# Starting TensorE's attention loop at step 0, on zeroed buffers, in a decode kernel that streams 186 MB

## The chip, the cores and the metric

The kernel runs on one core of a Trainium2 chip. The metric is the device time of one execution in microseconds (us), as the median of several. The profile is one further execution. Its span leaves out some 1.8 us that the device time includes.

The engines have short names in the profile. PE is TensorE, PEld its weight loads, DVE VectorE, ACT ScalarE, POOL GpSimd and SP SyncE, which issues the loads here. A core has 16 DMA engines, which carry out the loads.

## The reference, cut to what matters

One token goes through a transformer block with adaptive layer norm. All weights and the cache are read once, in bf16.

```python
mod = (silu(c) @ w_mod).reshape(1, 6, 1, -1)            # w_mod 1024 x 6144
h = layernorm(x) * (1 + ca) + sa
q = h @ wq                                              # wq 1024 x 4096, 32 heads of 128
scores = q . k_cache * 128 ** -0.5                      # 4 kv heads, 65,536 keys of 128, 8 query heads each
o = softmax(scores) . v_cache
x = x + ga * (o @ wo)
h = layernorm(x) * (1 + cb) + sb
x = x + gb * ((gelu(h @ w_gate) * (h @ w_up)) @ w_down) # F = 3584
```

K and V are 67 MB each, and the weights 51 MB.

## The kernel before

SyncE issues every load in one fixed order into ten buffers ("slots") of 2 MB: Wmod, Wq, then 32 K chunks and 32 V chunks, then Wo, gate, up and down. K chunk i uses slot i % 4, and V chunk j slot 4 + j % 4. A load is issued once TensorE has released the slot's earlier content:

```python
def issue_ready():
    while issued[0] < len(loads):
        j = loads[issued[0]]
        if j.prev is not None:
            if j.prev.freed is None:
                return
            SP.wait(j.prev.freed)
        sp.dma_start(j.view, j.src).then_inc(j.tok[0], 16)
        issued[0] += 1
```

The attention is a pipeline over 32 chunks. In step i TensorE transposes K chunk i (`T`, four groups of 16 tiles), multiplies chunk i-1 by q (`QK`), and multiplies V chunk i-2 by the softmax weights (`PV`). Steps 0 to 3 are unrolled code, because chunks -1 and -2 don't exist. Steps 4 to 31 are a hardware loop of 7 passes with 4 steps each, on TensorE alone. The other engines' code is fully unrolled. Steps 32 and 33 are unrolled again.

```python
FIRST, LAST = SITES, NC                     # 4, 32
[...]
def QK(b):
    j = i - 1
    if not 0 <= j < NC:
        return
[...]
PE.wait(t1, v_negi, v_q)
for i in range(FIRST):
    pe_step(i)
    others_step(i)
it0, it1 = FIRST // SITES, LAST // SITES
with nc.Fori(it0, it1, engines=OrderedEngineSet([pe.engine]), head_slot={pe.engine: 0}) as it:
    [...]
    for i in range(FIRST, FIRST + SITES):
        pe_step(i)
```

The products with Wmod, Wq, Wo, gate, up and down (`matvec`) take one matmul for each 128 x 128 block of the weights. The block is the stationary operand and one activation column moves.

## Time and profile before

| | before |
|---|---|
| time, median of 3 | 443.99 us (443.78 to 444.12) |
| span of the profile | 442.7 us |
| load queue (q1), share of 16 DMA engines' span | 98.5% |
| TensorE busy | 335.0 us, 76% |
| VectorE, ScalarE, GpSimd busy | 164.8, 143.1, 3.8 us |
| instruction queue (q8) | 25 packets, 0.41 MB |

The page of the kernel before gives the DMA queues with packets, MB and share of the 16 engines' span:

```profile
q1 hardware_dynamic: 15328, 185.61, 98.5%
q8 instruction: 25, 0.41, 0.3%
HBM read 185.60 MB, written 0.00 MB: 419 GB/s over the span
```

The table of stretches gives, for each: its bounds, its length, the busy time of PE, PEld, DVE, ACT and POOL with instruction counts, then the granted clock, the DMA share and GB/s. Three stretches of the kernel before:

```profile
0.00:10.00 10.00, 2.06 (x52) 1.92 (x52) 1.40 (x11) 1.46 (x2) 3.21 (x20) 1.00 0.81 317
60.00:70.00 10.00, 9.20 (x180) 8.64 (x178) 7.31 (x7) 1.88 (x1) 0.00 (x0) 1.00 1.01 429
200.00:240.00 40.00, 37.72 (x785) 37.02 (x784) 19.31 (x30) 17.86 (x73) 0.00 (x0) 0.71 1.01 432
```

The loads run at a share of 1.0 from 10 us on, at 420 to 436 GB/s. TensorE is nearly as busy in the attention (37.7 of 40 us in the last line), so the page's 76% hides a close second bound. The loads still come first: TensorE waits 15 times for a V chunk, 20.9 us in all.

In SyncE's timeline each line is one load, with its start and the length of the issue. These are the first loads of the kernel before that had to wait for the attention (K4, V2, K5, V3):

```profile
64.39 0.33 SPq L212 DMA_DIRECT2D slot<-in_A_k_cache_dram  x1
64.76 0.43 SPq L212 DMA_DIRECT2D slot<-in_A_v_cache_dram  x1
70.41 0.33 SPq L212 DMA_DIRECT2D slot<-in_A_k_cache_dram  x1
70.78 0.43 SPq L212 DMA_DIRECT2D slot<-in_A_v_cache_dram  x1
```

The last pieces of the chain of waits before (start, length, what) show how the kernel ends. The last down-projection load lands at 439.23 us, and 3.4 us of small work follow:

```profile
414.49 24.74 DMA slot<-in_B_w_down_dram
439.23 0.05 issue
439.28 0.60 PE kt_ps L316 x16
```

### The profile page before, as it was taken

What the parts mean: (1) busy time and instruction counts of PE and PEld (TensorE: products, weight loads), DVE (VectorE), ACT (ScalarE), POOL (GpSimd) and SP (SyncE); (2) the same over time, 40 slices, a digit from 0 to 9 for tenths busy, and PEclk for the clock granted to TensorE, in tenths of its full rate; (3) what the DMA queues carried; (4) which work ended last, traced back from release to release, by engine and by line L of the source; (5) the groups of instructions that cost most, each with busy time, mean ns of one, the idle gap of its engine ahead of it and who ended that gap; (6) DMA issues with size and microseconds to landing.
All of it is one profiled execution on the core that took longest, in us unless ns stands there. A gap on an engine that the chain in (4) does not pass through costs nothing.

```text
span 442.7 us, 16779 instructions
## 1 busy us (share of the span) xinstructions
PE 335.0 (76%) x7849; PEld 325.2 (73%) x7849; DVE 164.8 (37%) x282; ACT 143.1 (32%) x548; POOL 3.8 (1%) x21
## 2 busy tenths in 40 slices
PE   1333468898979899989899988979898974654434
PEld 1333458898979899979799987969898964654434
DVE  1000046544536445544644644554544443210000
ACT  1000013444444333634533453543343562000000
POOL 2000000000000000000000000000000000000000
PEclk9999999867788956967955996895967785555555
DMA  8999999999999999999999999999999999999994
GB/s 329 429 423 426 434 431 426 429 427 421 432 429 432 426 427 437 432 429 428 434 434 430 429 429 433 431 434 429 429 434 431 432 429 428 423 424 424 427 425 177
DMA packets 15392, 186.08 MB, mean 420 GB/s; under 512 B 1536, under 2 KB 1536, under 8 KB 3840
## 3 DMA queue, kind: packets, MB, share of 16 engines
q1 hardware_dynamic: 15328, 185.61, 98.5%
q8 instruction: 25, 0.41, 0.3%
q14 instruction: 7, 0.06, 0.0%
q10 hardware_dynamic: 32, 0.00, 0.0%
HBM read 185.60 MB, written 0.00 MB: 419 GB/s over the span
## 4 chain that ended last, share of the span: by engine, by line
DMA 75%; PE 20%; issue 2%; DVE 1%; SPq 1%; ACT 1%
DMA slot<-in_A_v_cache_dram 55%; PE kt_ps L417 9%; DMA slot<-in_A_wq_dram 8%; DMA slot<-in_B_w_up_dram 6%; DMA slot<-in_B_w_down_dram 6%; PE b L481 5%; PE sc_ps L437 3%; PE kt_ps L316 1%; SPq L212 1%; PE b L461 1%; ACT p_sb L547 1%; PE b L451 1%; DVE kt_sb L612 0%; PE b L621 0%; DVE zs L597 0%
## 5 line engine op out<-in xcount | busy, mean ns | idle before, releaser
L417 PE MATMUL kt_ps<-ident,slot 128*128 128x128 bf16 x2048 | 171.9, 252 | 4.9 <-DMA slot<-in_A_k_cache_dram 3.0
L516 DVE COPY kt_sb<-kt_ps 128x2048 bf16<-128x2048 bf16 x96 | 117.5, 1225 | 100.0 <-PE kt_ps L417 99.7
L417 PEld LDWEIGHTS kt_ps<-ident,slot 128*128 128x128 bf16 x2048 | 148.6, 114 | 6.6 <-issue 4.2
L516 ACT ACTIVATE kt_sb<-kt_ps 128x2048 bf16<-128x2048 bf16 x32 | 60.1, 1878 | 217.7 <-PE kt_ps L417 217.7
L481 PE MATMUL b<-p_sb,slot 128*128 128x8 bf16 x2048 | 71.0, 167 | 29.5 <-DMA slot<-in_A_v_cache_dram 20.9
L481 PEld LDWEIGHTS b<-p_sb,slot 128*128 128x128 bf16 x2048 | 65.1, 100 | 32.2 <-DMA slot<-in_A_v_cache_dram 22.2
L547 ACT ACTIVATE p_sb<-sc_ps,mneg 128x64 bf16<-128x64 f32 x256 | 83.6, 560 | 5.7 <-DVE mneg L542 5.7
L547 ACT ACTIVATION_READ_ACCUMULATOR p_sb<-sc_ps,mneg 128x1 f32 x256 | 77.2, 364 | 0.0
L437 PE MATMUL sc_ps<-q_buf,kt_sb 128*128 128x8 bf16 x2048 | 67.4, 167 | 0.1
L437 PEld LDWEIGHTS sc_ps<-q_buf,kt_sb 128*128 128x128 bf16 x2048 | 65.1, 100 | 0.2 <-issue 0.2
L316 PE MATMUL kt_ps<-h_col,slot 128*128 128x1 bf16 x448 | 16.2, 172 | 16.9 <-DMA slot<-in_B_w_up_dram 9.1
L316 PEld LDWEIGHTS kt_ps<-h_col,slot 128*128 128x128 bf16 x448 | 15.6, 118 | 17.6 <-DMA slot<-in_B_w_up_dram 9.4
L316 PE MATMUL sc_ps<-s_col,slot 128*128 128x1 bf16 x384 | 11.5, 165 | 15.8 <-DMA slot<-in_w_mod_dram 15.8
L535 DVE TENSOR_REDUCE m_col<-sc_ps 128x8 f32<-128x512 f32 x32 | 21.8, 681 | 4.4 <-PE sc_ps L437 4.4
L316 PEld LDWEIGHTS sc_ps<-s_col,slot 128*128 128x128 bf16 x384 | 11.0, 105 | 16.4 <-DMA slot<-in_w_mod_dram 16.4
L540 DVE TENSOR_REDUCE mg<-b 8x1 f32<-8x128 f32 x32 | 8.9, 279 | 34.4 <-PE b L451 34.4
L316 PE MATMUL sc_ps<-h_col,slot 128*128 128x1 bf16 x256 | 7.4, 165 | 12.6 <-DMA slot<-in_A_wq_dram 12.6
L316 PEld LDWEIGHTS sc_ps<-h_col,slot 128*128 128x128 bf16 x256 | 7.1, 104 | 12.9 <-DMA slot<-in_A_wq_dram 9.3
L461 PE MATMUL b<-negi,mg 8*128 8x8 f32 x64 | 15.0, 304 | 0.4 <-DVE mg L540 0.4
L461 PEld LDWEIGHTS b<-negi,mg 8*128 8x128 f32 x64 | 12.0, 233 | 2.6 <-DVE mg L540 0.6
L316 PE MATMUL kt_ps<-u_col,slot 128*128 128x1 bf16 x224 | 6.6, 165 | 9.6 <-DMA slot<-in_B_w_down_dram 9.6
L316 PEld LDWEIGHTS kt_ps<-u_col,slot 128*128 128x128 bf16 x224 | 6.3, 104 | 9.9 <-DMA slot<-in_B_w_down_dram 6.8
(74 smaller groups left out, 63.2 us busy)
## 6 DMA issues: line engine op xcount, KB each, us to landing
slot<-in_A_k_cache_dram SPq DMA_DIRECT2D x32, 2048.0 KB, 29.6
slot<-in_A_v_cache_dram SPq DMA_DIRECT2D x32, 2048.0 KB, 33.2
slot<-in_w_mod_dram SPq DMA_DIRECT2D x8, 1536.0 KB, 19.0
slot<-in_A_wq_dram SPq DMA_DIRECT2D x4, 2048.0 KB, 37.0
slot<-in_A_wo_dram SPq DMA_DIRECT2D x4, 2048.0 KB, 34.7
slot<-in_B_w_gate_dram SPq DMA_DIRECT2D x4, 1792.0 KB, 39.4
slot<-in_B_w_up_dram SPq DMA_DIRECT2D x4, 1792.0 KB, 29.0
slot<-in_B_w_down_dram SPq DMA_DIRECT2D x3, 2048.0 KB, 30.4
```

Of the source, the lines that this page charges most:

```text
L212: sp.dma_start(j.view, j.src).then_inc(j.tok[0], 16)
L316: ins = pe.matmul(bank[:, j:j + 1], w, rhs[:, k0 + kk:k0 + kk + 1], start=first, stop=True, skip_group_check=True,)
L417: ins = pe.transpose(kt_ps[:, half * 2048 + t * P:half * 2048 + (t + 1) * P], j_k[i].view[:, b * TB + t, :], ident[:, :],)
L437: ins = pe.matmul(sc_ps[:, base + n * REP:base + (n + 1) * REP], kt_sb[:, j % 2, n, :], q_buf[:, j % SITES, :], start=True, stop=True,)
L451: ins = pe.transpose(b6[0:REP, 32:32 + P], m_col[:, j % 2, :], identf[:, :]) if emit else None
L461: ins = pe.matmul(b6[:, 256:256 + REP], mg8[:, j % 2:j % 2 + 1].to_broadcast([REP, P]), negi[:, :], start=True, stop=True,)
L481: ins = pe.matmul(b7[:, s * REP:(s + 1) * REP], j_v[j].view[:, n, :], p_sb[:, s, n, :], start=(n == 0), stop=(n == CH - 1),)
L516: ev[i % SITES][b].done(act.activation(dst, src, ACT.Copy) if E_ is AC else dve.tensor_copy(dst, src))
L535: m1[s].done(dve.tensor_reduce(m_col[:, j % 2, :].unsqueeze(2), scv, AX.X, ALU.max))
L540: m2[s].done(dve.tensor_reduce(mg8[:, j % 2:j % 2 + 1], b6[0:REP, 32:32 + P], AX.X, ALU.max))
L547: ins = act.activation(p_sb[:, s, :, h], scv[:, h, :], ACT.Exp, bias=mneg[:, j, h:h + 1], scale=scale, accum_out=z_all[:, j, h:h + 1],)
```

## The change

The intent is a shorter TensorE program. The loop covers steps 0 to 31 in 8 passes, and the four unrolled steps ahead of it go. In the first pass, chunks -1 and -2 are buffers of zeros: half of `kt_sb`, two of the four places of `p_sb`, and half of `m_col` and of `mg8`. V chunks -2 and -1 are whatever lies in slots 6 and 7. These hold the first two Wq loads, which therefore may not be overwritten until steps 0 and 1 have read them (times zero). Results of the first pass that no one needs are written over later. The diff, cut to its core:

```diff
--- before
+++ after
@@ loads planned
-        j_k, j_v = {}, {}
+        j_k, j_v = {}, {-2: j_q[0][0], -1: j_q[1][0]}
@@ constants on GpSimd
         v_const = GP.done(ins)
+        GP.wait(v_const)
+        pool.memset(kt_sb[:, 1, :, :], 0.0)
+        pool.memset(p_sb[:, SITES - 2:SITES, :, :], 0.0)
+        pool.memset(m_col[:, 1, :], 0.0)
+        v_zero = GP.done(pool.memset(mg8[:, 1:2], 0.0))
@@ matvec(..., held=())
-                release(jb, tok)
+                if jb not in held:
+                    release(jb, tok)
@@ the Wq product
-        v = matvec(acc_bank["q"], with_view(j_q), h_col, (v_h,), HQ)
+        v = matvec(acc_bank["q"], with_view(j_q), h_col, (v_h,), HQ, held=(j_v[-2], j_v[-1]))
@@ range of the loop
-        FIRST, LAST = SITES, NC
+        FIRST, LAST = 0, NC
@@ T, QK, MT, MB, PV: the guard (five times alike; cut)
-                if not 0 <= j < NC:
+                if j >= NC:
                     return
@@ PV
-                            b7[:, s * REP:(s + 1) * REP], j_v[j].view[:, n, :], p_sb[:, s, n, :],
+                            b7[:, s * REP:(s + 1) * REP], kv_view(slots[SITES + s])[:, n, :], p_sb[:, s, n, :],
@@ ahead of the loop
-        PE.wait(t1, v_negi, v_q)
-        for i in range(FIRST):
-            pe_step(i)
-            others_step(i)
+        PE.wait(t1, v_negi, v_q, v_zero)
[... two waits, in T and PV, lose their "i >= 1" and "j >= 1" ...]
```

TensorE's program so loses 576 matmuls and a few small ones, each with a weight load. No other engine's order changes, except for the four memsets on GpSimd.

More of the change, by code (lines that the diff above doesn't have):

```diff
@@ L304, in emit_all, with matvec @@
         v_s = DVE.done(dve.tensor_tensor(s_col[:, :], b6[:, 0:KD], sg_col[:, :], ALU.mult))
-        def matvec(bank, jobs, rhs, ready, nblk, pick=None, first=True):
+        def matvec(bank, jobs, rhs, ready, nblk, pick=None, first=True, held=()):
             PE.wait(*ready)
@@ L404, in T @@
             def T(b):
-                if not 0 <= i < NC:
+                if i >= NC:
                     return
@@ L411, in T @@
                     pwait(ev[s][b - 2], i, it)
-                elif i >= 1:
+                else:
                     pwait(ev[(i - 1) % SITES][b + 2], i - 1, it)
@@ L447, in MT @@
                 j = i - 1
-                if not 0 <= j < NC:
+                if j >= NC:
                     return
@@ L455, in MB @@
                 j = i - 1
-                if not 0 <= j < NC:
+                if j >= NC:
                     return
@@ L468, in PV @@
                 j = i - 2
-                if not 0 <= j < NC:
+                if j >= NC:
                     return
@@ L474, in PV @@
                     pwait(ex[s], j, it)
-                    if j >= 1:
-                        pwait(oc[(j - 1) % SITES], j - 1, it)
+                    pwait(oc[(j - 1) % SITES], j - 1, it)
                 ins = None
```

## The prediction

> **What bounds the kernel now.** The load queue. The page gives it 98.5% of the 16 DMA engines' span; the table of stretches shows a DMA share of 1.00 to 1.02 from 10 to 420 us, at 421 to 436 GB/s. 185.6 MB at about 429 GB/s is 432.6 us (estimate); the rest of 443 us is the start, slower transfer in the first 10 us (317 GB/s), a ragged end, and 3.5 us after the last down-projection landing (439.2 us). [...]TensorE is busy 76% and waits 15 times for a V chunk (20.9 us): it keeps catching up.
>
> **What the change does.**
> - Removes four unrolled steps from TensorE's program: 4 x 64 transposes, 3 x 64 score and 2 x 64 value matmuls, 576 in all, each with a weight load. The loop runs 8 times instead of 7.
> - Adds in steps 0 and 1 work on zeros: 64 score and 128 value matmuls. A group of 16 lasts 0.4 us at full clock (timeline, 74 to 80 us), so 12 groups are 4.8 us; with small ones about 5.5 us of TensorE time between 59 and 80 us.
> - Adds memsets on GpSimd, 9,216 elements per partition in the large two. 128 elements took 0.21 us and 252 took 0.31 us, so about 8 us, from 3.7 to 12 us (estimate). The layer norm's power op on that engine moves from 9.2 to 12 us, but is first needed at 35.8 us: free.
> - Holds the slots of the first two Wq loads until steps 0 and 1 end. Before, K4/V2 were issued at 64.4/64.8 us, K5/V3 at 70.4/70.8. I expect about 67/68 and 74/76 us.
>
> **How much is on the critical path.** The issue delay isn't: chunks issued at 60 to 75 us land a median 27 (K) and 31 us (V) later, because they wait in the queue. A delay of 3 to 5 us leaves no gap. TensorE's added 5.5 us is eaten where it would have waited for V.
> What can move the end is DMA work. The instruction queue fetched 25 packets, 0.41 MB, 0.3% of the engines' span, about 0.9 us each (0.3% of 442.7 x 16 / 25). [...]1,152 instructions fewer are 4 or 5 blocks: 4 us of one engine, 0.26 us of all 16. If the slowest engine loses one block, the end comes up to 0.9 us earlier. The 1.9 us "issue" wait at 127 us may shift, off the path.
>
> **Predicted:** 443.5 us, 442.3 to 444.8 (8 in 10). Faster by over 2%: 1%; within 2%: 97%; slower: 2%.
>
> **What would show the steps right or wrong.** DMA share stays at 1.0 in every 10 us stretch of 10 to 420 us; K4/V2 and K5/V3 issue 2 to 6 us later in the SyncE timeline; instruction packets fall from 25 to 20 or 21; the chain of waits is again mostly DMA, ending on a down-projection load 3.5 us before the end; GpSimd busy rises from 3.8 to about 12 us; TensorE busy rises by 4 to 7 us; V waits in 60 to 100 us shrink.
>
> **What would make it wrong.** A loop entry that stalls TensorE for over 15 us, so that the queue runs dry; the held slots delaying V2 until the engines idle; or instruction blocks refetched in each pass, adding DMA work. An idle gap of all DMA engines between 60 and 110 us would be the sign.

(The runs show 4 blocks fewer for these 1,152 instructions (25 to 21), and 37 more for 9,216 (25 to 62). The sum came to 443.5 us, which is 444.0 before less some 0.5 us for the blocks.)

## The result, and the profile after

The first comparison gave 443.96 us (443.8 to 444.03, 6 runs) against 443.88 us for the kernel before (6 runs), a ratio of 1.000, interval 0.9987 to 1.0013. On two other occasions, with 5 runs each against 9 of before, it was 0.9999. The intervals are 95% intervals. Ratios in this document are the mean time of one kernel's fast runs over the mean of the other's of the same rounds, so not quite the ratio of the quoted medians. Every result was right unless the text says it was wrong.

The page after, DMA queues:

```profile
q1 hardware_dynamic: 15328, 185.61, 98.6%
q8 instruction: 21, 0.34, 0.3%
HBM read 185.60 MB, written 0.00 MB: 420 GB/s over the span
```

There are four instruction packets fewer, as intended, and the load queue is unchanged. Two stretches after, where the first pass runs:

```profile
60.00:70.00 10.00, 10.00 (x202) 9.95 (x202) 3.67 (x3) 1.47 (x1) 0.00 (x0) 1.00 1.01 429
70.00:80.00 10.00, 7.80 (x201) 7.58 (x199) 4.71 (x6) 2.56 (x4) 0.00 (x0) 0.99 1.00 426
```

No DMA time is lost, although the loads are issued later. SyncE's timeline after, K4, V2, K5 and V3:

```profile
68.52 0.33 SPq L212 DMA_DIRECT2D slot<-in_A_k_cache_dram  x1
69.42 0.33 SPq L212 DMA_DIRECT2D slot<-in_A_v_cache_dram  x1
76.00 0.33 SPq L212 DMA_DIRECT2D slot<-in_A_k_cache_dram  x1
79.20 0.33 SPq L212 DMA_DIRECT2D slot<-in_A_v_cache_dram  x1
```

That is 4.1, 4.7, 5.6 and 8.4 us later than before. Part of it is not matmul work. TensorE's timeline after (start, length, group, idle time before it in brackets) has two waits whose releaser the profile does not show:

```profile
59.92 1.86 PE L425 MATMUL kt_ps<-ident,slot 128*128 128x128 bf16 x16 [4.22 <-issue]
78.84 0.33 PE L488 MATMUL b<-p_sb,slot 128*128 128x8 bf16 x7 [2.15 <-issue]
```

The corresponding first group before, and a wait of the same kind that the kernel before has at 127 us:

```profile
58.78 4.25 PE L417 MATMUL kt_ps<-ident,slot 128*128 128x128 bf16 x48 [3.04 <-DMA slot<-in_A_k_cache_dram]
129.36 0.53 PE L481 MATMUL b<-p_sb,slot 128*128 128x8 bf16 x15 [1.92 <-issue]
```

The first group of transposes starts at 59.9 us instead of 58.8, and there is a stop of 2.15 us in step 1 that the unrolled code did not have there.

The DMA records of the traces show what happens beside such waits. In the kernel after, instruction blocks (16 KB pieces of a program, on queue q8) landed at 58.3, 77.3, 89.8 and 96.2 us, and 1.3 to 1.6 us after each of them a wait of this kind ended (4.22, 2.15, 0.62 and 2.03 us long). Blocks that landed at 64.3, 71.0 and 83.7 us had no such wait behind them. The 1.92 us of the kernel before ended 1.5 us after a block. From 100 to 360 us, where the kernel after fetches one block in all, no such wait is longer than 0.6 us. So TensorE probably waits there for its own instructions; no run tested it.

The head has a surprise. VectorE's timeline before and after, between 7.3 and 7.8 us and between 7.5 and 11.9 us:

```profile
7.30 0.17 DVE L301 COPY x_col<-b 128x8 f32<-128x8 f32 x1 [4.83 <-ACT th_col L299]
7.39 0.16 DVE L302 TENSOR_SCALAR sg_col<-th_col 128x8 f32<-128x8 f32 x1
7.58 0.17 DVE L304 TENSOR_TENSOR s_col<-b,sg_col 128x8 bf16<-128x8 f32 x1
```

```profile
7.52 0.17 DVE L308 COPY x_col<-b 128x8 f32<-128x8 f32 x1 [5.05 <-ACT th_col L306]
7.60 4.09 DVE L309 TENSOR_SCALAR sg_col<-th_col 128x8 f32<-128x8 f32 x1
11.72 0.17 DVE L311 TENSOR_TENSOR s_col<-b,sg_col 128x8 bf16<-128x8 f32 x1
```

The same TENSOR_SCALAR on 8 columns takes 4.09 us instead of 0.16. GpSimd's timeline after shows what ran beside it:

```profile
3.78 6.93 POOL L294 MEMSET kt_sb<- 128x8192 bf16 x1
10.64 0.96 POOL L295 MEMSET p_sb<- 128x1024 bf16 x1
11.57 0.09 POOL L297 MEMSET mg<- 8x1 f32 x1
```

VectorE's operation ends at 11.69 us, just after the last memset. The copy at 7.52 us, whose source is PSUM, was not held up. So the TENSOR_SCALAR was held up while GpSimd's memsets ran, for 4.09 us in all. It had to wait out the second memset too (10.64 to 11.60 us), not only the one that ran when it came. By what means a memset holds VectorE up, this trace does not show. The first Wmod product started at 12.5 us instead of 8.4.

The end of the chain of waits after has the same shape as before:

```profile
414.06 24.73 DMA slot<-in_B_w_down_dram
438.80 0.05 issue
438.85 0.60 PE kt_ps L323 x16
```

So far: the loads bind, the delays don't show, and four blocks fewer gave nothing that can be measured.

### A closer look at the DMA engines

Each load is done by 16 DMA engines, and the trace has 16 completion records for it. Worked out from them: when the first engine finished its part of the last down-projection load, how much later the other engines did (us), and the same for a load in mid-attention.

```
                mid-attention (193 us)             last load
                first   spread to the last    first    spread to the last
before          192.7   3.94                  433.8    5.39
after           192.8   3.30                  434.1    4.72
```

A load is complete only when its last engine is (before, 433.85 + 5.39 = 439.24 us, and the chain's wait for the last load ended at 439.23), and the kernel ends with the last load. The engines end 5 us apart. The spread does not grow in the later passes of the loop, where no instruction blocks are fetched (before, it is 3.94 us at 193 us and 3.90 us at 339 us), so the loads alone keep the engines level. It grows in the head and the tail, where blocks are fetched (before, from 0.9 us at the first Wmod load to 3.6 at 115 us, and from 3.9 at 339 us to 5.4 at the last load). This suggested theories that the prediction did not have:

- **Theory A (the fullest engine).** Instruction blocks go round only some of the DMA engines, and each block delays its engine. With 8 such engines, 24 blocks before the last load (kernel before) are 3 each. 20 blocks (after) leave 3 on the fullest. The gain is then zero, not 0.26 us.
- **Theory B (in proportion).** Each block costs the kernel its share of the 16 engines. The change gained 0.26 us, or up to 0.75 us at the cost of a block found later, which is hidden by noise or given back.
- **Theory C.** Instruction fetches cost nothing, as they are hidden.
- A separate question is why TensorE's later start costs nothing: because the queue of loads already issued covers it (the prediction's reason), or because a loss and a gain happen to cancel.

### The profile page after: what moved, and what is told of

Read it like the earlier page. It is cut to its first block, busy times and chain, and to the rows that moved or that the text cites. A ratio compares the mean times of both kernels' runs of the same rounds, so it can differ in the third digit from the quotient of the medians.

```text
span 442.2 us, 17178 instructions
## 1 busy us (share of the span) xinstructions
PE 335.6 (76%) x8044; PEld 327.0 (74%) x8044; DVE 168.8 (38%) x282; ACT 143.0 (32%) x548; POOL 11.6 (3%) x25
## 4 chain that ended last, share of the span: by engine, by line
DMA 55%; PE 39%; issue 3%; DVE 1%; ACT 1%; SPq 1%
DMA slot<-in_A_v_cache_dram 30%; PE kt_ps L425 20%; PE b L488 8%; DMA slot<-in_A_k_cache_dram 8%; PE sc_ps L445 7%; DMA slot<-in_B_w_up_dram 7%; DMA slot<-in_B_w_down_dram 6%; DMA slot<-in_w_mod_dram 5%; PE b L469 2%; PE kt_ps L323 1%; PE b L459 1%; ACT p_sb L554 1%; SPq L212 1%; DVE kt_sb L616 0%; PE b L625 0%
## 5 line engine op out<-in xcount | busy, mean ns | idle before, releaser
L425 PE MATMUL kt_ps<-ident,slot 128*128 128x128 bf16 x2048 | 169.5, 249 | 4.9 <-issue 4.6
L425 PEld LDWEIGHTS kt_ps<-ident,slot 128*128 128x128 bf16 x2048 | 146.5, 113 | 6.0 <-issue 4.8
L488 PE MATMUL b<-p_sb,slot 128*128 128x8 bf16 x2176 | 75.1, 167 | 28.2 <-DMA slot<-in_A_v_cache_dram 16.3
L488 PEld LDWEIGHTS b<-p_sb,slot 128*128 128x128 bf16 x2176 | 68.7, 99 | 30.8 <-DMA slot<-in_A_v_cache_dram 17.3
L445 PE MATMUL sc_ps<-q_buf,kt_sb 128*128 128x8 bf16 x2112 | 69.2, 167 | 0.7 <-issue 0.6
L445 PEld LDWEIGHTS sc_ps<-q_buf,kt_sb 128*128 128x128 bf16 x2112 | 66.4, 99 | 0.8 <-issue 0.7
L323 PEld LDWEIGHTS sc_ps<-s_col,slot 128*128 128x128 bf16 x384 | 10.9, 105 | 12.1 <-DMA slot<-in_w_mod_dram 12.1
L549 DVE COPY mneg<-b 128x8 f32<-128x8 f32 x32 | 5.3, 166 | 22.1 <-PE b L469 22.1
L469 PEld LDWEIGHTS b<-negi,mg 8*128 8x128 f32 x66 | 12.1, 227 | 2.2
```

Source lines behind the costliest of these rows:

```text
L323: ins = pe.matmul(bank[:, j:j + 1], w, rhs[:, k0 + kk:k0 + kk + 1], start=first, stop=True, skip_group_check=True,)
L425: ins = pe.transpose(kt_ps[:, half * 2048 + t * P:half * 2048 + (t + 1) * P], j_k[i].view[:, b * TB + t, :], ident[:, :],)
L445: ins = pe.matmul(sc_ps[:, base + n * REP:base + (n + 1) * REP], kt_sb[:, j % 2, n, :], q_buf[:, j % SITES, :], start=True, stop=True,)
L469: ins = pe.matmul(b6[:, 256:256 + REP], mg8[:, j % 2:j % 2 + 1].to_broadcast([REP, P]), negi[:, :], start=True, stop=True,)
L488: ins = pe.matmul(b7[:, s * REP:(s + 1) * REP], kv_view(slots[SITES + s])[:, n, :], p_sb[:, s, n, :], start=(n == 0), stop=(n == CH - 1),)
L549: v_mc[j] = DVE.done(dve.tensor_copy(mneg[:, j, :], b6[:, 256:256 + REP]))
```

## The experiments

### Control: the changed kernel again

> Control: the changed kernel itself, on the chip of the next three. Both theories: 443.9 us, ratio to before 1.000 within 0.002. The spread between first and last engine landing of one chunk in mid-run about 3.3 us.

Measured: 443.99 us against 444.27, ratio 0.9999 (0.9986 to 1.0013), mid-attention spread 3.3 us. As expected.

### Many more blocks: 28 unrolled steps

```diff
-        FIRST, LAST = SITES, NC
+        FIRST, LAST = NC - SITES, NC
```

> The kernel before with 28 instead of 4 steps unrolled ahead of the loop (loop of one pass): 9,216 TensorE instructions more, about 36 more instruction blocks of 16 KB (25 to about 61). Theory A (loads saturate the DMA engines, blocks go to only 8 of the 16, and the engine with most of them ends last: ceil(60/8) = 8 instead of 3 blocks, 0.93 us each): +4.6 us, 448.5, and the landing spread grows all through the attention. Theory B (blocks cost all 16 engines alike): 36 x 0.93 / 16 = +2.1 us, 446.0. Theory C (fetches are hidden and cost nothing): 443.9.

Measured: 451.15 us against 444.27, ratio 1.0155, so +6.9 us. All three theories missed the size. B's 2.1 and C's 0 are far off, and A had the cost of a block too low. The queues of this run's page:

```profile
q1 hardware_dynamic: 15328, 185.61, 97.3%
q8 instruction: 62, 1.02, 0.8%
```

The trace says why. In this kernel 40 blocks were fetched between 100 and 360 us. Each took 0.93 us on average, and in all 40 cases a 16 KB load packet that started as the block ended took about 1.1 us instead of 0.61. Together a block sets its engine back by 1.42 us (1.41 to 1.52). And it is always the same eight engines. The records do not name the engines, but the split into two groups shows it. These are the 16 completion times of one load after the first of them, in us, sorted, for five loads of this kernel:

```
first at
  46.7   0.00 0.01 0.20 0.25 0.30 0.33 0.37 0.38   0.46 0.49 0.64 0.77 1.09 1.86 1.99 2.11
 119.7   0.00 0.36 0.38 0.48 0.64 0.75 1.06 1.10   1.71 1.73 3.23 3.37 3.38 3.39 3.51 3.59
 241.3   0.00 0.37 0.38 0.49 0.77 1.05 1.09 1.19   5.99 6.04 6.10 6.12 6.19 6.29 6.34 7.84
 338.5   0.00 0.37 0.38 0.49 0.78 1.09 1.91 2.38   8.86 8.89 8.95 9.01 9.06 9.16 9.17 9.22
 433.9   0.00 0.38 0.53 0.82 0.96 1.06 1.89 2.33  10.20 10.22 10.25 11.84 11.90 12.00 12.01 12.07
```

Eight engines keep their places within 2.4 us. The other eight fall behind together, one step of about 1.4 us after another, to 10 to 12 us. The first engine finishes the last load at 433.9 us, as in the kernel before (433.8). So the extra blocks do nothing to the engines that take none. They cost 1.4 us a round on the eight that take them, and the kernel ends with the fullest of these. That blocks go round eight engines in turn shows in the fetches themselves: in order of time the first eight in this trace took 934, 931, 924, 960, 962, 954, 881 and 882 ns, and the same pattern repeats every eight blocks to the end, with a few near 1,050 ns.

### Fewer blocks, wrong result

```diff
-                    for j in range(nblk):
+                    for j in range(0, nblk, W):          # W = 4 for Wmod, Wq, Wo, gate; 1 for up, down
-                            bank[:, j:j + 1], w, rhs[:, k0 + kk:k0 + kk + 1],
+                            bank[:, j:j + W], w, rhs[:, k0 + kk:k0 + kk + 1].to_broadcast([P, W]),
```

> Wrong result on purpose: the changed kernel with only every fourth block-matmul (4 columns wide) in the Wmod, Wq, Wo and gate products: the loads are the same, the TensorE program is 840 matmuls shorter, 21 blocks become 14 or 15. The up and down products, after which the kernel ends, are untouched. Theory A: the fullest engine has 2 blocks instead of 3: -0.9 us, 443.0. Theory B: 6.5 x 0.93 / 16 = -0.4 us, 443.5. Theory C: 443.9.

Measured: 14 blocks, 442.94 us against 444.27, ratio 0.9968 (0.9954 to 0.9981). Against the control of the same rounds (443.99) it is 1.05 us faster, 1.3 us by the means. A, as corrected, says one round of 1.4 us less. The first engine ended at 433.8 us and the last 3.9 us later (4.7 in the control). Theory C is out, both ways.

### Taking load off the late engines by splitting transfers

```diff
+            if j.split:                                   # the last two gate loads
+                sp.dma_start(j.view[0:112], j.src[0:112]).then_inc(j.tok[0], 16)
+                sp.dma_start(j.view[112:120], j.src[112:120]).then_inc(j.tok[0], 16)
+                sp.dma_start(j.view[120:128], j.src[120:128]).then_inc(j.tok[0], 16)
```

> The changed kernel with the last two gate loads each split in three: rows 0-111, 112-119 and 120-127. [...]Theory A, if the blocks go to the upper 8: [...]-1.1 us, 442.9, spread at the end from 4.7 to about 2.6 us. Theory A, if they go to the lower 8: +1.1 us, spread about 6.8 us. Theory B, with a spread that has another, mixed cause: +0.5 to +1.1 us.

(An assumption about which engines a transfer of 8 rows uses, and the shift of 1.1 us of work from one half of the engines to the other that was worked out from it: the forecasts rest on it. No trace shows it, as the traces do not name the engines; nor do they show an "upper" or a "lower" half.)

Measured: 456.32 us, ratio 1.0274, so +12.2 us. No theory had that. The spread at the end was 5.9 us, between the two forecasts, but with packets slowed as below the run says nothing about which engines take the blocks. The table of stretches shows the cost where these two loads run:

```profile
390.00:400.00 10.00, 4.04 (x112) 3.88 (x112) 1.00 (x6) 0.00 (x0) 0.55 (x1) 0.50 1.03 243
400.00:410.00 10.00, 2.02 (x56) 1.94 (x56) 0.00 (x0) 0.00 (x0) 0.00 (x0) 0.50 1.02 216
```

The engines are busy all the time, at half the rate. In the trace, the 7 KB packets of 400 to 410 us took a median 529 ns, and in the changed kernel 272. Split into transfers of 112, 8 and 8 rows, this data moved more slowly than in one transfer of 128 rows. Why was not tried further.

### Two delays of TensorE ahead of the loop

```diff
         PE.wait(t1, v_negi, v_q, v_zero)
+        zf = kt_sb[:, 1, 0:8, :].rearrange("p a b -> p (a b)").bitcast(dt.float32)
+        for _ in range(7):                                # 28 in the second
+            pe.matmul(sc_ps[:, 512:1024], identf[:, :], zf, start=True, stop=True)
```

> The changed kernel with 7 dummy fp32 matmuls of 512 columns on TensorE just before the loop, [...]so that its first pass starts about 10 us later still. Theory A (TensorE is off the critical path as long as the queue has loads): after the change K4 was issued at 68.5 us and the queued loads last until the first engine has V1 at about 81 us; K4 at 78 to 79 us still comes in time: 444 us, ratio to before 1.000 to 1.003. Rival theory (TensorE's delays add up to the end, and the change gained as much elsewhere as its 4 to 8 us cost): +8 to +10 us, 453.

Measured: 444.32 us against 444.28, ratio 1.000. The delay came out smaller than meant. The dummies took 8.3 us (56.6 to 64.9), and TensorE then ran the first step faster (a group of 16 transposes took 1.06 us instead of 1.86), so K4 was issued at 70.9 us, 2.4 us after the changed kernel's 68.5. That is too little to test the lead, but it costs nothing.

> The same with 28 dummy matmuls, so that the first pass starts about 25 us later than in the changed kernel. Theory A: K4 is issued at about 94 us, the engines run dry from 81 us on and stand idle some 13 to 16 us, which comes back in the time: 457 to 461 us. Rival theory: +25 us, 469. If the lead were larger than 25 us, nothing: 444.

Measured: 452.24 us against 444.28, ratio 1.0183, so +8.0 us. SyncE's timeline and the stretches of this run:

```profile
88.55 0.33 SPq L212 DMA_DIRECT2D slot<-in_A_k_cache_dram  x1
```

```profile
75.00:80.00 5.00, 5.00 (x13) 2.29 (x12) 0.00 (x0) 0.00 (x0) 0.00 (x0) 1.00 1.01 429
80.00:85.00 5.00, 5.00 (x72) 3.48 (x71) 1.46 (x2) 0.00 (x0) 0.00 (x0) 1.00 0.23 98
85.00:90.00 5.00, 5.00 (x142) 4.95 (x139) 2.22 (x2) 1.44 (x1) 0.00 (x0) 1.00 0.27 56
90.00:95.00 5.00, 5.00 (x146) 5.00 (x144) 3.70 (x4) 0.43 (x1) 0.00 (x0) 1.00 0.87 370
```

K4 was issued at 88.6 us, 20.0 us after the changed kernel's, and the queue had run dry at about 81 us. So 20 us of delay cost 8, and about 12 us of lead were left in the changed kernel. The rule that delays add up is out: it wanted 20. The loss is smaller than expected partly because the delay was shorter (20, not 25 us), and partly because of the engines' spread. While the queue was dry, the late engines caught up: against the changed kernel the first engine's end moved by 9.5 us (434.1 to 443.6), but the spread at the end fell from 4.7 to 3.1 us. So by its first engine the changed kernel's lead was 10.5 us, and the rest of the 12 is spread made good. Theory A explains this second part, and B has no place for it.

### The memsets later

```diff
-        GP.wait(v_const)            # ahead of the layer norm
+        GP.wait(v_hn1)              # the same four memsets after it
         pool.memset(kt_sb[:, 1, :, :], 0.0)
```

> The changed kernel with the four memsets after the first layer norm's power op instead of ahead of it. Expected: the 4.09 us TENSOR_SCALAR on DVE at 7.6 us is back to 0.16 us and the first Wmod product starts at 8.4 us as before, not at 12.5, because GpSimd's 6.9 us memset no longer holds DVE off; the time is unchanged, 444.0, as the Wmod loads set the pace until 35 us. If the 4 us at the head did matter: up to -4 us, 440.

Measured: 444.18 us against 444.28, ratio 0.9997 (0.9982 to 1.0012). VectorE's timeline of this run:

```profile
7.45 0.16 DVE L304 TENSOR_SCALAR sg_col<-th_col 128x8 f32<-128x8 f32 x1
```

The operation is back to 0.16 us, with the 6.93 us memset at 10.2 us, after it. The first Wmod product started at 8.46 us. The memset was what held VectorE off, and the 4 us were free.

### Eight unrolled steps

```diff
-        FIRST, LAST = SITES, NC
+        FIRST, LAST = 2 * SITES, NC
```

> The kernel before with 8 instead of 4 steps unrolled: 1,536 TensorE instructions, 6 blocks of 16 KB more, so 30 instead of 24 before the last load. 62 blocks cost 6.9 us, a landing spread that grew by 1.4 us with each round of 8 blocks. Theory A: 30 blocks over 8 engines make a 4th round on 6 engines: +1.4 us, spread at the end 6.8 us. Theory B (cost in proportion to blocks, 6.9 us / 37 each): 6 x 0.19 = +1.1 us - too close to tell from A by time alone, but B has the spread unchanged.

Measured: 32 blocks, one more than planned, 445.38 us against 444.28, ratio 1.0025 (1.0011 to 1.0038), so +1.1 us. The spread at the end was 6.2 us (5.4 in the kernel before). By the time alone A and B can't be told apart here, as said beforehand. The larger spread is on A's side.

### A version with fewer blocks and a right result

The Wmod and Wq products are turned round. The activation column stands in the array, padded with zeros so that the result lands on partition 0, 32, 64 or 96, and 512 weight columns move. Small matmuls with a selection of the identity then turn the rows into columns. The memsets are late, as above.

```diff
+                for kk in range(nk):
+                    for g in range(4 * nb):
+                        b, r = divmod(g, 4)
+                        ins = pe.matmul(
+                            bank[:, b * 512:(b + 1) * 512], E[:, k0 + kk, 96 - 32 * r:96 - 32 * r + P],
+                            view[:, kk, g * 512:(g + 1) * 512],
+                            start=first[b], stop=True, skip_group_check=True,
+                        )
[...]
+            for c in range(4 * nb):
+                ins = pe.matmul(out_ps[:, 4 * c:4 * c + 4], rows_sb[:, c * P:(c + 1) * P], sel, start=True, stop=True)
-        v_mod = DVE.done(dve.tensor_copy(mod_sb[:, :], acc_bank["mod"][:, 0:MD]))
+        v_mod = matvec_rows(kt_fp, 3, with_view(j_mod), Em, (v_s, t1), b7, mod_sb[:, :])
```

> A version meant to beat both, with a right result: the changed kernel with late memsets, and the Wmod and Wq products turned round (the activation column as the stationary operand, 512 weight columns moving, then small matmuls that turn rows into columns): 160 + 20 matmuls for 640, so about 17 instruction blocks instead of 21 and 16 instead of 20 before the last load. Theory A (blocks go round 8 engines and the fullest one ends the kernel; 1.36 us a round): 2 rounds instead of 3, 442.7 to 443.0, ratio to before 0.997, first engine of the last load at 433.9 us, spread 3.9 us. Theory B (in proportion, 0.17 to 0.19 us a block): -0.7 us, 443.4. If the longer Wq product delays the attention by more than about 10 us, the queue runs dry and it is slower.

Measured: 442.77 us (442.62 to 443.02) against 444.12, ratio 0.9968 (0.9954 to 0.9981), result right. The page:

```profile
span 441.1 us, 16299 instructions
q8 instruction: 17, 0.28, 0.2%
```

The first engine ended at 433.9 us and the last 3.7 us later. TensorE was busy for 355.7 us, 20 us more than in the changed kernel, and K4 was issued at 70.3 us, within the lead. This version beats both kernels by about 1.4 us (0.3%), with more TensorE work and fewer instructions.

### Half of V, wrong result

```diff
-                j_v[j] = plan_load(kv_src(vh, j), kv_view,
+                j_v[j] = plan_load(kv_src(vh, j)[:, 0:CH // 2, :], lambda t: kv_view(t)[:, 0:CH // 2, :],
-                            b7[...], kv_view(slots[SITES + s])[:, n, :], p_sb[:, s, n, :],
+                            b7[...], kv_view(slots[SITES + s])[:, n % (CH // 2), :], p_sb[:, s, n, :],
```

> Wrong result on purpose: the changed kernel loading only half of each V chunk (each half used twice), 33.5 MB less, TensorE's work the same. If the loads bind and TensorE had room, the 78 us of loads would go: 366. I expect TensorE to become the bound soon, as it is 90 to 95% busy in the attention now: the attention (59 to 373 us) shrinks to about the sum of TensorE's busy time there, 295 us, so 425 to 435 us.

Measured: 402.56 us (2 runs), so -41.6 of the 78 us of loads taken away. That is more than I expected. (The check of the result did not catch the wrong V.) This run from 59 to 330 us, then the changed kernel from 59 to 373 us:

```profile
59.00:330.00 271.00, 254.50 (x6073) 249.15 (x6074) 148.19 (x224) 131.74 (x499) 0.00 (x0) 0.92 0.93 370
59.00:373.00 314.00, 283.56 (x6430) 277.55 (x6431) 154.09 (x235) 140.89 (x544) 0.00 (x0) 0.82 1.01 431
```

TensorE is busy 94% of this stretch and waits for no K or V chunk any more (16.3 us for V in the changed kernel), so TensorE is the second bound, as supposed. The loads are close behind, with a share of 0.93. My size was off because I took TensorE's busy time as fixed. The granted clock was 0.92 here, and 0.82 in the changed kernel. An estimate from these: 283.6 us of busy time at 0.82 are 253 us at 0.92, and 254.5 were measured. What sets the clock was not tested.

### The control once more

> Control: the changed kernel again, in the rounds of the row version. Theory A: ratio to before 1.000 (3 rounds of blocks both). Theory B: four blocks fewer, -0.7 us, ratio 0.998.

Measured: 444.12 us against 444.12, ratio 0.9999 (0.9985 to 1.0012). B's 0.998 is just outside the interval, in both controls and in the first comparison.

### All kernels by their blocks

| kernel | blocks | fullest engine by A | spread at the last load | time | ratio to before |
|---|---|---|---|---|---|
| fewer blocks (wrong result) | 14 | 2 | 3.9 us | 442.94 | 0.9968 |
| row version | 17 | 2 | 3.7 us | 442.77 | 0.9968 |
| after (controls) | 21 | 3 | 4.7 and 5.2 us | 443.99, 444.12 | 0.9999, 0.9999 |
| before | 25 | 3 | 5.4 us | 443.88 to 444.28 | 1 |
| 8 unrolled | 32 | 4 | 6.2 us | 445.38 | 1.0025 |
| 28 unrolled | 62 | 8 | 12.1 us | 451.15 | 1.0155 |

The kernels with the short delay and with the late memsets, 21 blocks as well, had spreads of 5.3 and 5.1 us. The fullest engine's count is the blocks but the last one or two, which come when the last load is nearly over, divided by 8 and rounded up. From 2 to 8 blocks the spread grows by 8.3 us, 1.4 us each. The time follows in the same steps: about -1.4, 0, +1.1 and +6.9 us.

## Why the prediction was right, and where it was not

The number and the main reason hold. Point by point:

- **The loads bind, and TensorE's delay is covered by the queue.** Right. The DMA share stayed at 0.99 to 1.03 in every 10 us stretch from 10 to 120 us and was 1.01 on average after that, to 420 us, and the chain ended on a down-projection load 3.4 us before the end. The long delay put a number on the cover: a further 20 us cost 8, so 12 us were left after the change had used 4. The rival, a cancelling loss and gain, would have shown the full 20.
- **Issue times.** K4, V2 and K5 came 4.1 to 5.6 us later, inside the predicted 2 to 6. V3 came 8.4 us later, because of the stop of 2.15 us in step 1. The prediction had the step's matmuls and the possibility that the 1.9 us "issue" wait at 127 us would move, but did not add the two.
- **TensorE busy up by 4 to 7 us.** Not seen: 335.0 to 335.6 us. The added work is there (score and value matmuls 67.4 + 71.0 to 69.2 + 75.1 us, so +5.9). The transposes took 2.4 us less in the after profile, at a mean granted clock of 0.795 against 0.774. The change's work and the clock's luck can't be told apart in the sum of busy times. The waits for V shrank as predicted, from 1.2 us to none in 60 to 100 us, and from 20.9 to 16.3 us in all.
- **The memsets are free.** Right in time (the late version gave 0.9997), and GpSimd's busy time went to 11.6 us as estimated. But the argument looked at GpSimd alone. The memset held up a VectorE operation for 4 us (4.09 instead of 0.16) and moved the first Wmod product by 4 us. It was free only because the Wmod loads take until 34 us.
- **"1,152 instructions fewer are 4 or 5 blocks: 4 us of one engine, 0.26 us of all 16."** The count is right (25 to 21). This is the term that was mis-sized. A block costs its engine 1.42 us, not 0.9, because the load packet behind it is slow too (about 1.1 us instead of 0.61 in the version with 28 unrolled steps). Only 8 of the 16 engines take blocks (in that version 8 ended the last load 10.2 to 12.1 us after the first engine, and the others within 2.4), and only the fullest engine's count matters. That count was 3 before and 3 after, so the gain is zero. The predicted 443.5 with its 0.5 us of gain was off by this, inside the range and inside the noise.

What stays open: which 8 engines take the blocks, why the packet after a block is slow, whether the stop of 2.15 us in the first pass is a wait for an instruction block, as the landing just before its end suggests, and why the split transfers ran at half rate. An attempt to shift load from the late engines by other means was not made. Whether step 0 could run without holding the Wq slots was not tried, since TensorE would then read a slot while a load writes it.

## What to carry to other kernels

Where loads bind, ask how long a delay of the compute engine stays covered by the loads already issued. Here a further 2.4 us cost nothing, and a further 20 us cost 8. Count that lead in microseconds (here some 16 us before the change and 12 after, by the time lost) and spend it where it buys something. A load was done here by 16 DMA engines and ended with the slowest, 3.7 to 12.1 us after the first, so look at the spread of their completions as well as at the mean share. Small extra transfers that always fall on the same engines, as the instruction blocks did here, count by rounds and not by bytes: from 2 to 8 blocks on the fullest engine the spread grew by 1.4 us each. Before calling an engine's added work free, look at what the other engines do in the same microseconds (here a memset on GpSimd cost VectorE 4 us).
